# Moving the hi and lo halves of split operands, and the sums of exponentials, in a hand-ordered attention and MoE kernel

## The chip, the core and the metric

The kernel runs on one core of one Trainium2 chip. Its time is the device time of one execution in microseconds (us). TensorE (PE) multiplies matrices; its weight loads are listed apart as PEld. VectorE (DVE), ScalarE (ACT) and GpSimd (POOL) do the elementwise work, and SyncE (SP) issues the DMAs. Each engine works through its own instructions in order, and an instruction waits on semaphores until what it needs has been done by the others.

## The reference

Attention over pooled keys and values comes first, then a gated MoE layer with a third weight matrix:

```python
k_p = k.reshape(B, H, Sp, 8, D).mean(axis=3)          # B 8, H 8, S 576, D 64, Sp 72
v_p = v.reshape(B, H, Sp, 8, D).mean(axis=3)
scores = (1 / sqrt(D)) * q @ k_p^T
attn = exp(scores - max(scores)); attn = attn / (sum(attn) + 1e-9)
x = (attn @ v_p) as [B * S, H * D]                    # 4608 x 512
a = x @ w1; b = x @ w2                                # 512 x 1024 each
out = ((a * b) @ w3) @ w_out                          # 1024 x 1024, 1024 x 512
```

All inputs and the output are float32.

## The kernel before

**Split operands.** PE multiplies operands in a rounded form of float32 (`F32R`). For accuracy an operand is split into a hi part, which is a cast, and a lo part, which is the operand minus its hi part. A product is then three matmuls: hi times hi, hi times lo, lo times hi (`PASSES`). The cast runs on ACT, the subtraction on DVE, or on POOL for most blocks of w1 and w2. `split` (L151 to 153) issues both, one right behind the other. The same pair is written out for the transposed probabilities (`pt_post`, L486 and 487), for x (`av_post`, L510 and 511), for the product g = a * b (`b_post` L546 and `g_lo` L551), and for the leftover keys (`soft3`, L451 and 453).

**Stages.** First w3 and w_out are converted and multiplied into one matrix W (`w_mm`, L586). Then the 4608 tokens pass in 12 chunks of 384. For each chunk and each of 8 column blocks j, PE makes a = x w1 (`a_mm`), b = x w2 (`b_mm`, both L525), and adds g W to three accumulators (`out_mm`, L560). ACT copies a out of PSUM (`a_post`, L535), and DVE multiplies it with b (`b_post`, L545). Beside the MoE of one chunk the attention of the next is made. A chunk has three tiles of 128 tokens, or four of 96. Per tile the steps are: scores in two halves of four heads (`s_mm`, L404); minimum, subtraction, exponential and sum (`soft1`, L420 to 430); normalization (`soft2`, L439 to 442); leftover keys R (`soft3`); transposes of E and R on PE (`pt_mm` L464, `ptr_mm` L474); their copies (`pt_post`, `ptr_post`). Per pair of heads the product with the values follows (`av_mm`, L499 to 502). In five early tiles (`SOFT_ACT`) ACT makes exponential and sum in one (L430); all other tiles sum on DVE (L426).

**Weights.** The raw words of w1 and w2 are converted beside the first MoE chunk: L135 on ACT, L140 and L148 on DVE, then the split into `hl` (L152, L153).

**PSUM.** Five banks hold accumulators (`a`, `b`, `o0` to `o2`). Three banks, all called `att`, serve everything else: scores, transposes, attention products. A bank is free for the next use when its last reader is done.

**What sets the order.** A hand-written plan. `at(kind, k, fn, ...)` enters a step for slot k; a slot is about one group of MoE matmuls. The steps are sorted by the whole number of the slot, then by kind (loads L, elementwise steps P, MoE matmuls M, attention matmuls A), then by the fraction of k, then by entry. The sorted steps are issued one by one, so the order on each engine follows from the plan. `K0` is the slot 20, `M0` the slot 36 of the first MoE matmul.

Of the kernel before, what the change touches and what calls it, by code (L numbers as in the profile page):

```python
# [12 lines left out]
ALU = mybir.AluOpType  # L13
AX = mybir.AxisListType
# [4 lines left out]
def kernel(  # L19
# [14 lines left out]
    nc = tc.nc  # L34
# [3 lines left out]
    P = 128  # L38
# [3 lines left out]
    KR = KP - KM  # L42
# [45 lines left out]
    def f(ap):  # L88
        return ap.bitcast(F32)
# [56 lines left out]
    def conv_b(r, z):  # L146

        nc.vector.scalar_tensor_tensor(  # L148
            out=r, in0=z.bitcast(I32), scalar=3, in1=r, op0=ALU.logical_shift_left, op1=ALU.bitwise_or)

    def split(src, hi, lo, eng=nc.vector):  # L151
        nc.scalar.copy(out=hi, in_=src)  # L152
        eng.tensor_tensor(out=lo, in0=src, in1=f(hi), op=ALU.subtract)  # L153
# [207 lines left out]
    def pool_tree(t, dst):  # L361
        nc.gpsimd.tensor_tensor(out=t[:, :, 0:4], in0=t[:, :, 0:4], in1=t[:, :, 4:8], op=ALU.add)  # L362
        nc.gpsimd.tensor_tensor(out=t[:, :, 0:2], in0=t[:, :, 0:2], in1=t[:, :, 2:4], op=ALU.add)  # L363
        nc.gpsimd.tensor_tensor(out=dst, in0=t[:, :, 0], in1=t[:, :, 1], op=ALU.add)
# [12 lines left out]
    def prep_vr(b):  # L377
        m = p1.tile([P, 2, D], F32, tag="vrm", name="vrm")
        hi = p1.tile([P, 2, D], F32R, tag="vrh", name="vrh")
        pool_tree(stage.pop(("vr", b)), m)  # L380
        nc.scalar.copy(out=hi, in_=m)

        nc.scalar.activation(out=f(hi), in_=f(hi), func=AF.Copy, scale=msk[:, 0:1])
        nc.scalar.activation(out=m, in_=m, func=AF.Copy, scale=msk[:, 1:2])
        stage["vrp", b] = f(hi), m
# [25 lines left out]
    def soft1(n, t, half):  # L411

        b, off, nt = tok_tiles(n)[t]
        if half == 0:
            Et[n, t] = p2.tile([P, H, KP], F32, tag="E", name="E")
            Mt[n, t] = [p2.tile([P, H], F32, tag=tag, name=tag) for tag in ("mx", "sm")]
        E, (mx, sm) = Et[n, t], Mt[n, t]
        hs = slice(4 * half, 4 * half + 4)
        sv = Sp.pop((n, t, half))[:nt, :4 * KP].rearrange("p (h k) -> p h k", k=KP)
        nc.vector.tensor_reduce(out=mx[:nt, hs], in_=sv, axis=AX.X, op=ALU.min)  # L420
        if (n, t) not in SOFT_ACT:
            nc.vector.tensor_tensor(  # L422
                out=E[:nt, hs], in0=sv,
                in1=mx[:nt, hs].unsqueeze(2).broadcast_to([nt, 4, KP]), op=ALU.subtract)
            nc.scalar.activation(out=E[:nt, hs], in_=E[:nt, hs], func=AF.Exp, scale=-1.0)  # L425
            nc.vector.reduce_sum(out=sm[:nt, hs], in_=E[:nt, hs], axis=AX.X)  # L426
            return
        for i in range(4):
            h = 4 * half + i
            nc.scalar.activation(  # L430
                out=E[:nt, h], in_=sv[:, i], func=AF.Exp, scale=-1.0, bias=mx[:nt, h:h + 1],
                accum_out=sm[:nt, h:h + 1])
# [3 lines left out]
    def soft2(n, t):  # L436
        b, off, nt = tok_tiles(n)[t]
        E, sm = Et[n, t], Mt.pop((n, t))[1]
        nc.vector.tensor_scalar(  # L439
            out=sm[:nt], in0=sm[:nt], scalar1=1e-9, scalar2=float(POOL), op0=ALU.add, op1=ALU.mult)  # L440
        nc.vector.reciprocal(out=sm[:nt], in_=sm[:nt])
        nc.vector.tensor_tensor(
            out=E[:nt], in0=E[:nt], in1=sm[:nt].unsqueeze(2).broadcast_to([nt, H, KP]), op=ALU.mult)

    def soft3(n, t):
        b, off, nt = tok_tiles(n)[t]
        E = Et[n, t]
        R = Rt[n, t] = p2.tile([P, NPR, 2, 2, 2, KR], F32R, tag="R", name="R")
        er = E[:nt].rearrange("p (a h) (x e) -> p a (h x) e", h=2, e=KR)[:, :, 0:18:17, :]
        for dup in range(2):  # L450
            nc.scalar.copy(out=R[:nt, :, :, dup, 0], in_=er)  # L451
        for dup in range(2):
            nc.vector.tensor_tensor(
                out=R[:nt, :, :, dup, 1], in0=er, in1=f(R[:nt, :, :, dup, 0]), op=ALU.subtract)
# [23 lines left out]
    def pt_post(n, t):  # L478
        b, off, nt = tok_tiles(n)[t]
        if t == 0:  # L480
            PTh[n] = p1.tile([P, NPR, CH], F32R, tag="PTh", name="PTh")
            PTl[n] = p1.tile([P, NPR, CH], F32R, tag="PTl", name="PTl")
            PTr[n] = p1.tile([P, 2, CH], F32R, tag="PTr", name="PTr")
        pv = Tp.pop((n, t))
        hi, lo = PTh[n][:, :, off:off + nt], PTl[n][:, :, off:off + nt]
        nc.scalar.copy(out=hi, in_=pv[:, :, :nt])  # L486
        nc.vector.tensor_tensor(out=lo, in0=pv[:, :, :nt], in1=f(hi), op=ALU.subtract)

    def ptr_post(n, t):
        b, off, nt = tok_tiles(n)[t]  # L490
# [14 lines left out]
    def av_post(n, pr):  # L505
        if pr == 0:
            xT[n] = [xp.tile([P, NK, CH], F32R, tag=f"xT{s}", name=f"xT{s}") for s in range(2)]
        ps = Tp.pop((n, pr, "x"))[:, :CH]
        xh, xl = xT[n][0][:, pr], xT[n][1][:, pr]
        nc.scalar.copy(out=xh, in_=ps)  # L510
        nc.vector.tensor_tensor(out=xl, in0=ps, in1=f(xh), op=ALU.subtract)  # L511
# [28 lines left out]

    def b_post(m, j):
        g, ps = gt[m, j]
        gh = p2.tile([P, CH], F32R, tag="gh", name="gh")
        gl = p2.tile([P, CH], F32R, tag="gl", name="gl")
        nc.vector.tensor_tensor(out=g, in0=ps[:, :CH], in1=g, op=ALU.mult)  # L545
        nc.scalar.copy(out=gh, in_=g)  # L546
        gt[m, j] = (g, gh, gl)

    def g_lo(m, j):
        g, gh, gl = gt[m, j]  # L550
        nc.vector.tensor_tensor(out=gl, in0=g, in1=f(gh), op=ALU.subtract)  # L551
# [43 lines left out]


    plan = []

    def at(kind, k, fn, *args):


        plan.append((k // 1, "LPMA".index(kind), k % 1, len(plan), fn, args))

    def plan_att(n, s_at, ds, pt_at, av_at):


# [147 lines left out]
```

## Time and profile before

| | |
|---|---|
| median of 3 runs | 806.71 us (804.27 to 809.61) |
| profiled execution | 805.16 us, span 803.4 us |
| busy | PE 97%, PEld 90%, DVE 54%, ACT 36%, POOL 24% |
| mean granted clock of PE | 0.989 |
| first MoE matmul | 86.74 us after the start of the span |

A line of the profile names the source line, the engine, the operation, and the tiles as out<-in. In a timeline the first number is the start and the second the duration, in us; in square brackets stands how long the engine was idle just before and what ended that. In a group the count is followed by the busy time in us, the mean in ns, and the idle time before. A stretch A:B gives the busy time of PE, PEld, DVE, ACT and POOL, each with its number of instructions, then the clock granted to PE as a share of full speed, the DMA share and GB/s.

### The profile page before, as it was taken

The page shows a single profiled execution, that of the slowest core. Times are in us where ns is not written, and L with a number is a line of the kernel's source. Part 1 is how long each engine was busy: PE and PEld are TensorE (multiplying, and loading weights), DVE is VectorE, ACT ScalarE, POOL GpSimd, SP SyncE. Part 2 cuts the span into 40 slices and gives each one's busy share as a digit, 9 for nine tenths or more (in the row PEclk, how much of TensorE's full clock was granted, in tenths as well). Part 3 has the DMA queues.
Part 4 walks back from the last instruction along what each step waited for, and adds up shares of the span by engine and source line. Part 5 has one row for each costly group of instructions (what it writes and reads, how often), then busy time and mean ns, then how long its engine had stood idle before and what let it go on. Part 6 is the DMA issues. An engine that isn't in the chain of part 4 may idle for free.

```text
span 803.4 us, 11625 instructions
## 1 busy us (share of the span) xinstructions
PE 777.9 (97%) x4344; PEld 722.2 (90%) x4344; DVE 431.7 (54%) x873; ACT 288.0 (36%) x727; POOL 196.1 (24%) x234
## 2 busy tenths in 40 slices
PE   7899888999999999999999999999999999999998
PEld 6677777899999999999999999999999999999997
DVE  6968989465373375374374374474454455452112
ACT  5567565332243233242242333232242332332211
POOL 2155465107007302025008102034028020000000
PEclk8999999999999999999999999999999999999999
DMA  9988960045034030062043030071143110100101
GB/s 333 267 206 217 273 145 1 1 94 123 1 72 120 27 80 1 1 143 75 1 95 109 27 67 1 17 157 44 43 85 91 53 26 1 40 1 1 40 1 39
DMA packets 106632, 62.63 MB, mean 78 GB/s; under 512 B 73680, under 2 KB 90320, under 8 KB 106576
## 3 DMA queue, kind: packets, MB, share of 16 engines
q1 hardware_dynamic: 106576, 61.89, 30.1%
q8 instruction: 34, 0.56, 0.3%
q14 instruction: 22, 0.18, 0.1%
HBM read 52.43 MB, written 9.44 MB: 77 GB/s over the span
## 4 chain that ended last, share of the span: by engine, by line
PE 85%; DVE 7%; DMA 4%; issue 2%; ACT 2%; SPq 0%; DVEq 0%
PE o L560 24%; PE a L525 24%; PE b L525 23%; PE att L404 4%; PE o L586 2%; DMA st<-in_k_dram 2%; PE att L464 2%; DVE wb L140 1%; DVE wb L148 1%; PE att L501 1%; PE att L500 1%; PE att L502 1%; PE att L499 1%; PE att L474 1%; DMA raw<-in_moe_w_out_dram 1%
## 5 line engine op out<-in xcount | busy, mean ns | idle before, releaser
L525 PE MATMUL a<-xT,hl 128*128 128x384 f32 x1152 | 223.1, 342 | 0.0
L525 PE MATMUL b<-xT,hl 128*128 128x384 f32 x1152 | 220.3, 339 | 0.4 <-DVE Wc L153 0.4
L525 PEld LDWEIGHTS a<-xT,hl 128*128 128x128 f32 x1152 | 205.0, 190 | 4.9 <-POOL hl L153 0.2
L525 PEld LDWEIGHTS b<-xT,hl 128*128 128x128 f32 x1152 | 198.7, 188 | 0.8 <-DVE Wc L153 0.8
L560 PE MATMUL o<-Wc,gh 128*128 128x512 f32 x576 | 183.6, 400 | 0.0
L560 PEld LDWEIGHTS o<-Wc,gh 128*128 128x128 f32 x576 | 105.1, 189 | 17.3
L545 DVE TENSOR_TENSOR a<-b,a 128x384 f32<-128x384 f32 x96 | 53.1, 553 | 123.5 <-PE b L525 123.5
L362 POOL TENSOR_TENSOR st<-st 72x512 f32<-72x512 f32 (+1 forms) x53 | 73.0, 1377 | 173.2 <-DMA st<-in_k_dram 161.0
L560 PE MATMUL o<-Wc,gl 128*128 128x512 f32 x288 | 114.0, 396 | 0.0
L535 ACT COPY a<-a 128x384 f32<-128x384 f32 x96 | 46.1, 480 | 179.9 <-PE a L525 160.6
L546 ACT CAST gh<-a 128x384 fp32r<-128x384 f32 x96 | 49.2, 512 | 148.4 <-DVE a L545 148.4
L551 DVE TENSOR_TENSOR gl<-a,gh 128x384 fp32r<-128x384 f32 x96 | 59.4, 619 | 35.8 <-ACT gh L546 35.4
L375 POOL TENSOR_TENSOR vbd<-vm,vbd 64x256 fp32r<-64x256 f32 x16 | 13.3, 833 | 249.8 <-ACT vbd L374 248.2
L560 PEld LDWEIGHTS o<-Wc,gl 128*128 128x128 f32 x288 | 54.1, 188 | 12.5
L511 DVE TENSOR_TENSOR xT<-att,xT 128x384 fp32r<-128x384 f32 x48 | 26.5, 556 | 70.0 <-ACT xT L510 70.0
L426 DVE TENSOR_REDUCE sm<-E 128x4 f32<-128x288 f32 (+1 forms) x70 | 31.6, 451 | 46.3 <-ACT E L425 46.3
L404 PE MATMUL att<-kbd,qT 128*128 128x144 f32 (+1 forms) x320 | 52.1, 286 | 0.2 <-ACT E L430 0.2
L420 DVE TENSOR_REDUCE mx<-att 128x4 f32<-128x288 f32 (+1 forms) x80 | 36.0, 450 | 28.8 <-PE att L404 28.7
L425 ACT ACTIVATE E<-E 128x288 f32<-128x288 f32 (+1 forms) x70 | 31.1, 445 | 55.4 <-DVE E L422 55.4
L404 PEld LDWEIGHTS att<-kbd,qT 128*128 128x128 f32 (+1 forms) x320 | 46.6, 179 | 1.1 <-ACT E L430 0.5
L586 PE MATMUL o<-hl 128*128 128x512 f32 x144 | 42.3, 430 | 3.3 <-DVE hl L177 3.3
L363 POOL TENSOR_TENSOR st<-st 72x256 f32<-72x256 f32 (+1 forms) x53 | 41.8, 789 | 4.2
(87 smaller groups left out, 806.4 us busy)
## 6 DMA issues: line engine op xcount, KB each, us to landing
raw<-in_moe_w_dram SPq DMA_DIRECT2D x32, 512.0 KB
st<-in_k_dram SPq DMA_DIRECT2D x32, 288.0 KB
out_dram<-ob SPq DMA_DIRECT2D x35, 256.0 KB
st<-in_v_dram SPq DMA_DIRECT2D x32, 256.0 KB
qs<-in_q_dram SPq DMA_DIRECT2D x128, 48.0 KB
raw<-in_moe_w_out_dram SPq DMA_DIRECT2D x8, 512.0 KB
st<-in_v_dram SPq DMA_DIRECT2D x64, 64.0 KB
qs<-in_q_dram SPq DMA_DIRECT2D x96, 24.0 KB
```

Of the source, the lines that this page charges most:

```text
L362: nc.gpsimd.tensor_tensor(out=t[:, :, 0:4], in0=t[:, :, 0:4], in1=t[:, :, 4:8], op=ALU.add)
L363: nc.gpsimd.tensor_tensor(out=t[:, :, 0:2], in0=t[:, :, 0:2], in1=t[:, :, 2:4], op=ALU.add)
L404: nc.tensor.matmul(out=ps[:nt, 2 * KP * j:2 * KP * (j + 1)], lhsT=qT[n][:, pr, off:off + nt], rhs=kbd[b % 2][:, pr], start=True, stop=True,)
L420: nc.vector.tensor_reduce(out=mx[:nt, hs], in_=sv, axis=AX.X, op=ALU.min)
L426: nc.vector.reduce_sum(out=sm[:nt, hs], in_=E[:nt, hs], axis=AX.X)
L525: nc.tensor.matmul(out=o, lhsT=w12[j, w][sw][:, kt * P:(kt + 1) * P], rhs=x[sx][:, kt], start=(i == 0), stop=(i == 3 * NK - 1))
L535: nc.scalar.copy(out=a, in_=gt[m, j][:, :CH])
L545: nc.vector.tensor_tensor(out=g, in0=ps[:, :CH], in1=g, op=ALU.mult)
L546: nc.scalar.copy(out=gh, in_=g)
L551: nc.vector.tensor_tensor(out=gl, in0=g, in1=f(gh), op=ALU.subtract)
L560: nc.tensor.matmul(out=oacc[m][t], lhsT=(gh, gl)[sg][:, c], rhs=W[j][sw], start=(j == 0 and i == 0), stop=(j == NJ - 1 and i == 2))
L586: nc.tensor.matmul(out=wacc[h][it], lhsT=w3t[s][sa][:, it * P:(it + 1) * P], rhs=wo[j][sb], start=(j == 0 and i == 0), stop=(j == NJ - 1 a ...
```

## The change

The cast and the subtraction of a split become two steps. `late` issues the cast and stores the subtraction under a key; `lo` issues the stored subtraction where the plan says. This holds for w1 and w2, the transposed probabilities ("pt"), x ("x") and g ("g"). `soft3` is divided into casts (`soft3`) and subtractions (`soft4`), and `prep_vr` into additions on POOL and scalings on ACT (`prep_vr1`), which move to a later slot, as do the sums on POOL behind them. The two half sums of exponentials of a tile (L426) become one over all eight heads, issued in `soft2`. In the second chunk (n == 1) `soft2` and what follows it move by fractions of a slot. No matmul changes its place, nor any DMA.

```diff
+    def late(key, src, hi, lo, eng=nc.vector):
+        nc.scalar.copy(out=hi, in_=src)
+        los[key] = lo, src, f(hi), eng
+
+    def lo(*key):
+        sub(*los.pop(key))
...
-            nc.vector.reduce_sum(out=sm[:nt, hs], in_=E[:nt, hs], axis=AX.X)
             return
...
     def soft2(n, t):
+        if (n, t) not in SOFT_ACT:
+            nc.vector.reduce_sum(out=sm[:nt], in_=E[:nt], axis=AX.X)
...
     def b_post(m, j):
         g, ps = gt[m, j]
+        nc.vector.tensor_tensor(out=g, in0=ps[:, :CH], in1=g, op=ALU.mult)
+        gt[m, j] = g
+
+    def g_hi(m, j):
+        g = gt[m, j]
         gh = p2.tile([P, CH], F32R, tag="gh", name="gh")
         gl = p2.tile([P, CH], F32R, tag="gl", name="gl")
-        nc.vector.tensor_tensor(out=g, in0=ps[:, :CH], in1=g, op=ALU.mult)
-        nc.scalar.copy(out=gh, in_=g)
+        late(("g", m, j), g, gh, gl)
...
+    SL = (2, 3.1)
...
-            at("P", k + 2, soft2, n, t)
-            at("P", k + 3, soft3, n, t)
+            at("P", k + SL[n == 1], soft2, n, t)
+            at("P", k + 3 + 0.2 * (n == 1), soft3, n, t)
+            at("P", k + 3 + 0.45 * (n == 1), soft4, n, t)
...
+            at("P", k + 1 + 0.35 * (n == 1), lo, "pt", n, t)
...
-            at("P", av_at[pr] + 1, av_post, n, pr)
+            at("P", av_at[pr] // 1 + 1.1, av_post, n, pr)
+            at("P", av_at[pr] // 1 + 1.5, lo, "x", n, pr)
...
-        at("P", prep_r + 1, prep_vr2, b)
+        at("P", prep_r + 1.3, prep_vr1, b)
+        at("P", prep_r + 2.3, prep_vr2, b)
...
+            at("P", k + 4 + (0.75 if (j, w) in LO_DVE else 0), lo, "w12", j, w)
...
-            at("P", k + 2.5, g_lo, m, j)
+            at("P", k + 2.35, g_hi, m, j)
+            at("P", k + 2.9, lo, "g", m, j)
```

Three places show what that does to the queues. The first is DVE's queue when the first chunk's attention products come out, just ahead of the first MoE matmul. km is the fourth part of a batch's pooled keys, wb and raw belong to the conversion of w1 and w2, xT is x with its hi part as second input. Before:

```order
L319 TENSOR_REDUCE km<-st 72x128
L148 SCALAR_TENSOR_TENSOR wb<-wb 128x512
L511 TENSOR_TENSOR xT_980<-att,xT_979 128x384
L140 TENSOR_SCALAR wb<-raw 128x512
L153 TENSOR_TENSOR hl<-wb,hl 128x512
L511 TENSOR_TENSOR xT_980<-att,xT_979 128x384 x3
```

and now (all subtractions of a split have the line of `sub`, L152):

```order
L332 TENSOR_REDUCE km<-st 72x128
L148 SCALAR_TENSOR_TENSOR wb<-wb 128x512
L140 TENSOR_SCALAR wb<-raw 128x512
L152 TENSOR_TENSOR xT_982<-att,xT_981 128x384 x4
L152 TENSOR_TENSOR hl<-wb,hl 128x512
```

The first lo part of x has moved behind the conversion L140, and the other three ahead of the lo part of a block of w2.

The second place is DVE's queue at the end of the second chunk's attention, while the MoE of the first chunk is at j = 4. The scores' minimum mx and subtraction E are the last tile's second half. Before:

```order
L420 TENSOR_REDUCE mx<-att 96x4
L422 TENSOR_TENSOR E<-att,mx 96x288
L426 TENSOR_REDUCE sm<-E 96x4
L551 TENSOR_TENSOR gl<-a,gh 128x384
L439 TENSOR_SCALAR sm<-sm 96x8
L441 RECIPROCAL sm<-sm 96x8
L442 TENSOR_TENSOR E<-E,sm 96x576
L276 STREAM_TRANSPOSE qT<-qs 128x384
L487 TENSOR_TENSOR PTl<-att,PTh 128x4x96
L453 TENSOR_TENSOR R<-E,R 96x8x8 x2
```

and now:

```order
L437 TENSOR_REDUCE mx<-att 96x4
L439 TENSOR_TENSOR E<-att,mx 96x288
L152 TENSOR_TENSOR gl<-a,gh 128x384
L289 STREAM_TRANSPOSE qT<-qs 128x384
L152 TENSOR_TENSOR PTl<-att,PTh 128x4x96
L289 STREAM_TRANSPOSE qT<-qs 128x384
L456 TENSOR_REDUCE sm<-E 96x8
L457 TENSOR_SCALAR sm<-sm 96x8
L459 RECIPROCAL sm<-sm 96x8
L460 TENSOR_TENSOR E<-E,sm 96x576
L152 TENSOR_TENSOR R<-E,R 96x8x8 x2
```

The sum and the normalization have moved behind two transposes of q and the lo part of the third tile's probabilities, and R stands right behind the normalization.

The third place is ACT's queue at the same time. E are the last tile's exponentials in two halves, vrh and vrm the leftover values' scalings, gh the cast of g for j = 4. Before:

```order
L451 CAST R<-E 96x8x8 x2
L425 ACTIVATE E<-E 96x288
L381 CAST vrh<-vrm 128x128
L383 ACTIVATE vrh<-vrh,msk 128x128
L384 ACTIVATE vrm<-vrm,msk 128x128
L546 CAST gh<-a 128x384
L425 ACTIVATE E<-E 96x288
L152 CAST hl<-wb 128x512 x2
L486 CAST PTh<-att 128x4x96
```

and now (all casts of `late` have the line L162):

```order
L442 ACTIVATE E<-E 96x288
L471 CAST R<-E 96x8x8 x2
L442 ACTIVATE E<-E 96x288
L162 CAST hl<-wb 128x512
L398 CAST vrh<-vrm 128x128
L400 ACTIVATE vrh<-vrh,msk 128x128
L401 ACTIVATE vrm<-vrm,msk 128x128
L162 CAST gh<-a 128x384
L162 CAST hl<-wb 128x512
L162 CAST PTh<-att 128x4x96
```

The cast of g has moved behind the second half's exponential, a cast of a weight block and the three scalings.

More of the change, by code (lines that the diff above doesn't have):

```diff
@@ L149, in conv_b, with sub @@
             out=r, in0=z.bitcast(I32), scalar=3, in1=r, op0=ALU.logical_shift_left, op1=ALU.bitwise_or)
+    def sub(out, a, b, eng=nc.vector):
+        eng.tensor_tensor(out=out, in0=a, in1=b, op=ALU.subtract)
     def split(src, hi, lo, eng=nc.vector):
         nc.scalar.copy(out=hi, in_=src)
-        eng.tensor_tensor(out=lo, in0=src, in1=f(hi), op=ALU.subtract)
+        sub(lo, src, f(hi), eng)
+    los = {}
+    def late(key, src, hi, lo, eng=nc.vector):
[3 more added lines that the diff above has]
+        sub(*los.pop(key))
     def w_tiles(s):
@@ L236, in w12_split @@
         w12[j, w] = hl_cell(FREED[2 * j + w])
-        split(f(r), *w12[j, w], eng=nc.vector if (j, w) in LO_DVE else nc.gpsimd)
+        late(("w12", j, w), f(r), *w12[j, w], eng=nc.vector if (j, w) in LO_DVE else nc.gpsimd)
     def pieces(n):
@@ L380, in prep_vr, with prep_vr1 @@
         pool_tree(stage.pop(("vr", b)), m)
+        stage["vrp", b] = hi, m
+    def prep_vr1(b):
+        hi, m = stage.pop(("vrp", b))
         nc.scalar.copy(out=hi, in_=m)
@@ L443, in soft2, with rest_keys, soft4 @@
             out=E[:nt], in0=E[:nt], in1=sm[:nt].unsqueeze(2).broadcast_to([nt, H, KP]), op=ALU.mult)
+    def rest_keys(n, t):
+        nt = tok_tiles(n)[t][2]
+        return Et[n, t][:nt].rearrange("p (a h) (x e) -> p a (h x) e", h=2, e=KR)[:, :, 0:18:17, :]
     def soft3(n, t):
-        b, off, nt = tok_tiles(n)[t]
-        E = Et[n, t]
+        nt = tok_tiles(n)[t][2]
         R = Rt[n, t] = p2.tile([P, NPR, 2, 2, 2, KR], F32R, tag="R", name="R")
-        er = E[:nt].rearrange("p (a h) (x e) -> p a (h x) e", h=2, e=KR)[:, :, 0:18:17, :]
         for dup in range(2):
-            nc.scalar.copy(out=R[:nt, :, :, dup, 0], in_=er)
+            nc.scalar.copy(out=R[:nt, :, :, dup, 0], in_=rest_keys(n, t))
+    def soft4(n, t):
+        nt = tok_tiles(n)[t][2]
+        R = Rt[n, t][:nt]
         for dup in range(2):
-            nc.vector.tensor_tensor(
-                out=R[:nt, :, :, dup, 1], in0=er, in1=f(R[:nt, :, :, dup, 0]), op=ALU.subtract)
+            sub(R[:, :, :, dup, 1], rest_keys(n, t), f(R[:, :, :, dup, 0]))
     Tp = {}
@@ L484, in pt_post @@
         pv = Tp.pop((n, t))
-        hi, lo = PTh[n][:, :, off:off + nt], PTl[n][:, :, off:off + nt]
-        nc.scalar.copy(out=hi, in_=pv[:, :, :nt])
-        nc.vector.tensor_tensor(out=lo, in0=pv[:, :, :nt], in1=f(hi), op=ALU.subtract)
+        hi, lo_ = PTh[n][:, :, off:off + nt], PTl[n][:, :, off:off + nt]
+        late(("pt", n, t), pv[:, :, :nt], hi, lo_)
     def ptr_post(n, t):
@@ L509, in av_post @@
         xh, xl = xT[n][0][:, pr], xT[n][1][:, pr]
-        nc.scalar.copy(out=xh, in_=ps)
-        nc.vector.tensor_tensor(out=xl, in0=ps, in1=f(xh), op=ALU.subtract)
+        late(("x", n, pr), ps, xh, xl)
     PASSES = ((0, 0), (0, 1), (1, 0))
@@ L542, in b_post @@
         g, ps = gt[m, j]
+        nc.vector.tensor_tensor(out=g, in0=ps[:, :CH], in1=g, op=ALU.mult)
+        gt[m, j] = g
+    def g_hi(m, j):
+        g = gt[m, j]
         gh = p2.tile([P, CH], F32R, tag="gh", name="gh")
         gl = p2.tile([P, CH], F32R, tag="gl", name="gl")
-        nc.vector.tensor_tensor(out=g, in0=ps[:, :CH], in1=g, op=ALU.mult)
-        nc.scalar.copy(out=gh, in_=g)
+        late(("g", m, j), g, gh, gl)
         gt[m, j] = (g, gh, gl)
-    def g_lo(m, j):
-        g, gh, gl = gt[m, j]
-        nc.vector.tensor_tensor(out=gl, in0=g, in1=f(gh), op=ALU.subtract)
     def out_mm(m, j):
```

## The prediction

> **What bounds it now.** I read the page first: TensorE (PE) is busy for 97% of the span, VectorE (DVE) for 54%. The waits and the stages then say where that 97% leaves something to move. Waits of PE between 80 and 145 us, the only ones after 80 us:
>
> ```profile
> PE 777.9 (97%) x4344; PEld 722.2 (90%) x4344; DVE 431.7 (54%) x873; ACT 288.0 (36%) x727; POOL 196.1 (24%) x234
> ```
>
> ```profile
> PE att L474 <- ACT E L430: 4.7, 2, 3.9
> PE att L474 <- DVE E L422: 2.0, 1, 2.0
> PE att L474 <- DVE R L453: 1.7, 1, 1.7
> PE att L499 <- DVE xT L511: 1.6, 1, 1.6
> PE att L328 <- DVE km L319: 1.6, 1, 1.6
> PE b L525 <- DVE Wc L153: 0.4, 1, 0.4
> ```
>
> They make 12.0 us. Busy times of two stretches (us; PE, PEld, DVE, ACT, POOL, granted clock):
>
> ```profile
> 92.00:144.00 52.00, 41.87 (x224) 38.25 (x222) 47.81 (x75) 27.70 (x88) 29.86 (x26) 0.93 0.44 92
> 144.00:803.40 659.40, 655.49 (x3707) 617.38 (x3707) 310.99 (x675) 201.21 (x492) 131.96 (x163) 1.00 0.21 51
> ```
>
> So there are two kernels in one. From 144 us on PE runs without a wait for 659.4 us, and nothing that DVE does sooner can shorten that. From 92 to 144 us (first MoE chunk, attention of the second, and conversion of w1 and w2) DVE is busy for 47.81 of 52 us and PE only for 41.87. The last of PE's waits shows where the two meet, in order of time (start, duration):
>
> ```profile
> 141.74 2.09 DVE L453 TENSOR_TENSOR R<-E,R 96x64 fp32r<-96x64 f32 x2
> ...
> 143.97 0.36 PE L474 MATMUL att<-ident,R 96*128 96x96 f32 x2 [1.73 <-DVE R L453]
> ```
>
> I call this the gate: the transposes of R of the second chunk's last tile. PE's own work is the same before and after, in the same order. The new time is therefore the old one plus the shift of the gate, as long as PE does not wait behind it. The other waits lie ahead of the gate, and shortening them alone gives nothing. What counts is the length of DVE's queue up to R.
>
> **Part 1: the attention products of chunk 0.** Rows from 77 to 84 us:
>
> ```profile
> 77.71 0.41 DVE L140 TENSOR_SCALAR wb<-raw 128x512 int32<-128x512 int32 x1
> ...
> 82.47 1.55 POOL L362 TENSOR_TENSOR st<-st 72x512 f32<-72x512 f32 x1 [2.40 <-DMA st<-in_k_dram]
> 82.78 0.55 DVE L511 TENSOR_TENSOR xT<-att,xT 128x384 fp32r<-128x384 f32 x1
> 83.25 1.05 DVE L140 TENSOR_SCALAR wb<-raw 128x512 int32<-128x512 int32 x1
> ...
> 83.39 0.44 PE L499 MATMUL att<-PTh,vbd 128*128 128x384 f32 x1 [1.60 <-DVE xT L511]
> ```
>
> The fourth product waits for the first lo part of xT, which reads its PSUM bank last. That lo part now stands behind the L140. L140 takes 0.41 alone, but it took 1.05 beside POOL's addition and ended at 84.30, 0.28 after POOL's (82.47 + 1.55 = 84.02). Starting earlier it should end there again, so the lo part starts at 84.3, not 82.78: 1.5 us. Some 0.2 comes back, since the three other lo parts no longer stand behind the split of w2. I take **+1.3**; bounds +0.4 (L140 unhindered) and +1.5. The first a, the casts of W behind it and DVE, which waits for these, move along.
>
> The Trainium skill ("SBUF — State Buffer", Who interferes with whom) says that GpSimd shares a pair of SBUF ports with VectorE, locked for a whole instruction; tensor_scalar and operations with two SBUF inputs can want it, tensor_reduce never does. The L140 above agrees; by that rule the end at 84.3 holds, and the longer sum of part 2 is not stretched.
>
> **Part 2: DVE's queue from 92 us to the gate.** What goes are waits of DVE:
>
> ```profile
> DVE sm L426 <- ACT E L425: 2.0, 4, 0.5
> ...
> DVE gl L551 <- ACT gh L546: 0.9, 1, 0.9
> DVE wb L148 <- ACT wb L135: 0.8, 1, 0.8
> ```
>
> Each half tile's sum waited 0.5 for its exponentials; now other work stands between. **-3.7**, and what takes their place is priced anew below. Groups of DVE instructions from 92 to 144 us (count | busy, mean ns):
>
> ```profile
> L148 DVE SCALAR_TENSOR_TENSOR wb<-wb 128x512 int32<-128x512 int32 x11 | 11.6, 1052 | 0.9 <-ACT wb L135 0.8
> L140 DVE TENSOR_SCALAR wb<-raw 128x512 int32<-128x512 int32 x10 | 8.9, 890 | 0.0
> L442 DVE TENSOR_TENSOR E<-E,sm 96x576 f32<-96x576 f32 x4 | 4.7, 1164 | 0.1
> ...
> L426 DVE TENSOR_REDUCE sm<-E 96x4 f32<-96x288 f32 x4 | 1.8, 449 | 2.0 <-ACT E L425 2.0
> ...
> L276 DVE STREAM_TRANSPOSE qT<-qs 128x384 f32<-128x384 f32 x2 | 1.1, 564 | 0.0
> ```
>
> ```profile
> 96.30 0.67 DVE L148 SCALAR_TENSOR_TENSOR wb<-wb 128x512 int32<-128x512 int32 x1
> ...
> 118.86 0.76 DVE L442 TENSOR_TENSOR E<-E,sm 96x576 f32<-96x576 f32 x1
> ```
>
> Four sums of 288 (0.45 each) become two of 576. No row has that shape. Its bounds are 0.45 and 0.90; I take 0.75, by L442's 576 elements undisturbed: 2 x 0.75 - 4 x 0.45 = **-0.3**. One more transpose of q stands ahead of R: **+0.56**.
>
> New waits come from ScalarE (ACT), whose cast of g (gh) moves behind other work of its slot. ACT's groups from 92 to 144 us, then single rows:
>
> ```profile
> L152 ACT CAST hl<-wb 128x512 fp32r<-128x512 f32 x13 | 7.9, 616 | 0.0
> L135 ACT ACTIVATE wb<-raw 128x512 f32<-128x512 f32 x9 | 6.1, 672 | 0.0
> ...
> L546 ACT CAST gh<-a 128x384 fp32r<-128x384 f32 x5 | 2.6, 516 | 3.4 <-DVE a L545 3.4
> ...
> L425 ACT ACTIVATE E<-E 96x288 f32<-96x288 f32 x4 | 1.8, 444 | 8.5 <-DVE E L422 8.5
> L451 ACT CAST R<-E 96x64 fp32r<-96x64 f32 x8 | 1.6, 246 | 5.9 <-DVE E L442 5.9
> ```
>
> ```profile
> 111.53 0.32 ACT L430 ACTIVATE E<-att,mx 96x72 f32<-96x72 f32 x1 [2.73 <-DVE mx L420]
> ...
> 112.64 0.20 ACT L430 ACTIVATION_READ_ACCUMULATOR E<-att,mx 96x1 f32 x1
> ...
> 133.94 0.28 ACT L381 CAST vrh<-vrm 128x128 fp32r<-128x128 f32 x1
> ...
> 134.56 0.39 ACT L384 ACTIVATE vrm<-vrm,msk 128x128 f32<-128x128 f32 x1
> ```
>
> - lo of g(1): behind E come an exponential 0.44, an L135 0.67 and gh 0.52 on ACT, 1.6; on DVE one L140 covers 0.4 to 0.9: wait 1.0.
> - g(2): four exponentials 1.3 (111.53 to 112.84) and gh 0.5, covered by an L148 0.7: 1.0. Behind it the lo part of PT waits for its cast, which stands behind gh, L135 and an L152: 0.7.
> - g(3): the same, covered by an L148 and an L140: 0.6.
> - g(4): exponential 0.44, L152 0.62, the three scalings of vr 1.0 (133.94 to 134.95), gh 0.52, with nothing between on DVE: 2.6.
> - R of tiles 0, 2 and 3 now stands right behind E's scaling and waits for its own cast: 0.25 and 0.2 of handover, 1.4 in all.
>
> Together **+7.3**. Behind a waiting lo part everything of DVE queues up, the sums and R of the gate too.
>
> Against this stands POOL, busy for 29.86 of these 52 us. DVE's SBUF operations run longer beside it: L148 11 x (1.05 - 0.67), L140 10 x (0.89 - 0.41), L442 4 x (1.16 - 0.76), 10.6 us in these three. While DVE waits, POOL's work gets done, and stretches the next rows less. The added idle time is 7.3 - 3.7 = 3.6. Bounds 0 (POOL has nothing ready) and -7 (two thirds of the stretch); I take one for one, **-3.6**.
>
> **The rest.** Chunks 2 to 11 get the same moves. Their cover is the idle half of DVE; a later lo of g has this margin:
>
> ```profile
> 167.49 0.55 DVE L551 TENSOR_TENSOR gl<-a,gh 128x384 fp32r<-128x384 f32 x1
> ...
> 172.62 0.72 PE L560 MATMUL o<-Wc,gh 128*128 128x512 f32 x2
> ```
>
> It ends 4.6 us before its use, and is moved by under a slot of PE: nothing. POOL's VR sums a slot later and the hi casts bunched are not on the way. SP's queue is unchanged.
>
> **Sum.** 1.3 - 3.7 - 0.3 + 0.56 + 7.3 - 3.6 = +1.6 on the profiled execution's 805.16 (span 803.4 and 1.76 around it): **806.8**. The median shown, 806.71, is 1.55 above that execution; measured from there it would be 808.3. Under 1% (8 us) I count as no change.
>
> **A clock that could fall.** Three stretches of 3.41 or 4 us:
>
> ```profile
> 130.42:133.83 3.41, 1.45 (x11) 1.07 (x10) 3.10 (x6) 0.24 (x1) 1.91 (x3) 1.00 0.00 0
> ...
> 134.00:138.00 4.00, 4.00 (x16) 4.00 (x16) 3.39 (x8) 2.96 (x9) 2.26 (x5) 0.59 0.02 4
> ...
> 140.66:144.07 3.41, 1.68 (x11) 1.25 (x10) 3.41 (x6) 1.22 (x4) 2.00 (x2) 1.00 0.00 0
> ```
>
> After a stretch with PE busy for 1.45 us the clock halved for 3.4 us, which costs 1.7; the wait at the gate, with 1.68, just escaped. Ahead of the gate such a fall is hidden, behind it it counts in full.
>
> The Trainium skill ("TensorE: Matmul & The Clock Gate", What's actually happening) lets the clock drop after at least one idle window of about 3.4 us. Here 2 us of idleness was enough, so the trace is stricter. By the page nothing would be added at the gate, and rival B would be 810.4.
>
> **Rivals.**
> - A, faster: ACT, idle for half of this stretch, serves the casts in time. Then the 7.3 goes, and POOL may still interfere less: 1.3 - 3.7 - 0.3 + 0.56 = -2.1, with 3.4 of relief -5.5: **799.7**. For it speaks ACT's 27.70 of 52 us, against it that ACT is served in order and gh stands behind casts that wait for DVE. PE's waits of 12.0 cap it.
> - B, slower: POOL has nothing to do in DVE's new pauses, which come while ACT still makes its inputs. Relief 0: +5.2; and the wait before the gate, longer by the pause at g(4), leaves PE busy for under 1.5 of 3.4 us: +1.7. **812.1**. It decides where lo of g(4) ends more than 3 us later than now.
> - C: in later chunks a bank or a lo part comes late and PE waits 1 us in each of 11 chunks: 806.8 + 11 = **817.8**. Only the margin above speaks, against it.
>
> **Chances.** Forecast 0.60 (802 to 810), A 0.22 (796 to 802), B 0.14 (810 to 814), C 0.04. The range 798 to 812 leaves out a quarter of A, half of B and C, under 0.2. Faster by over 1%: 0.07, the lower third of A; slower by over 1%: 0.05, C and a sliver of B; within: 0.88.
>
> **What would show it.** Right: the sums' wait is gone, lo of g waits over 2 us at g(4), PE's fourth product starts about 1.5 us later than its cue, R of the last tile ends at 145 to 146, and no wait of PE follows. Wrong: R ends before 142 (A) or after 148 (B), or PE waits after 200 us (C).

## The result and the profile after

The changed kernel takes 800.58 us (median of 10 runs, 796.16 to 803.34) against 806.30 us for the kernel before on the same chip: a ratio of **0.9922, 95% interval 0.9901 to 0.9944**. It is faster by 0.8%, less than the 1% that I had called a change, but surely not the same, and not slower as forecast.

The page of the kernel after, busy times of the engines:

```profile
PE 778.0 (97%) x4344; PEld 721.4 (90%) x4344; DVE 418.9 (52%) x838; ACT 285.6 (36%) x727; POOL 195.5 (24%) x234
```

The stretches from the first a to the gate, and from the gate to the end (columns as before: PE, PEld, DVE, ACT, POOL, clock). Before:

```profile
86.74:143.97 57.23, 46.66 (x250) 42.65 (x249) 52.04 (x82) 32.95 (x98) 31.07 (x26) 0.94 0.50 116
143.97:803.40 659.43, 655.51 (x3707) 617.41 (x3707) 311.02 (x675) 201.21 (x492) 131.96 (x163) 1.00 0.21 51
```

and after:

```profile
88.88:140.79 51.91, 44.60 (x250) 39.19 (x249) 44.46 (x80) 32.95 (x98) 29.84 (x25) 1.00 0.48 100
140.79:800.20 659.41, 655.51 (x3707) 617.47 (x3707) 307.80 (x641) 199.02 (x493) 131.63 (x164) 1.00 0.21 51
```

Behind the gate nothing changed: 659.43 and 659.41. The stretch ahead of it became 5.32 shorter. DVE is busy there for 7.58 less (52.04 to 44.46) and idle for 2.26 more (5.19 to 7.45). ACT does the same work, POOL nearly. PE, busy for 2.06 less with the same matmuls, was granted the full clock throughout. PE's waits from the first a to the gate, after:

```profile
PE att L487 <- DVE E L460: 2.8, 3, 2.2
PE att L341 <- DVE km L332: 1.6, 1, 1.6
PE att L497 <- DVE R L152: 1.5, 4, 0.7
...
PE b L546 <- DVE Wc L152: 0.6, 1, 0.6
```

Where PE waited 4.7 and 2.0 for the exponentials and the subtraction, and 1.7 for R at the gate, it now waits 2.8 for the normalized E, and 1.5 for R, spread over four places. The end of the second chunk's attention, in order of time (DVE, and two rows of PE):

```profile
135.15 0.83 DVE L152 TENSOR_TENSOR gl<-a,gh 128x384 fp32r<-128x384 f32 x1 [2.35 <-ACT gh L162]
...
137.32 0.70 DVE L456 TENSOR_REDUCE sm<-E 96x8 f32<-96x576 f32 x1
...
140.11 0.52 PE L487 MATMUL att<-ident,E 96*128 96x96 f32 x4 [2.18 <-DVE E L460]
140.28 0.37 DVE L152 TENSOR_TENSOR R<-E,R 96x64 fp32r<-96x64 f32 x2 [0.31 <-ACT R L471]
...
140.79 0.36 PE L497 MATMUL att<-ident,R 96*128 96x96 f32 x2 [0.16 <-DVE R L152]
```

The wait of 2.35 at g(4) is there, as forecast, and still the gate comes 3.2 us earlier. R, which took 2.09, takes 0.37. DVE still comes last here: where PE waited 1.73 for R, it waits 2.18 for the normalized E, just ahead of the gate, and 0.16 for R.

Two more stretches belong to the account. From the first attention product of chunk 0 to the first a it was 7.24 us (79.50 to 86.74) and is 5.24 (83.64 to 88.88). Ahead of that product the change moves little, but single executions differ there by several us: it starts between 76.73 and 83.64 us in the 14 profiles of this study, without order by kernel. So I compare profiles from that product on. There the change brings 2.00 + 5.32 + 0.02 = 7.3 us; the medians say 5.7 (4.5 to 8.0 by the interval).

### The profile page after: what moved, and what is told of

The parts are those of the page before. It is cut to its first block, busy times and chain, and to the rows that moved or that the text cites. A ratio compares the mean times of both kernels' runs of the same rounds, so it can differ in the third digit from the quotient of the medians.

```text
span 800.2 us, 11632 instructions
## 1 busy us (share of the span) xinstructions
PE 778.0 (97%) x4344; PEld 721.4 (90%) x4344; DVE 418.9 (52%) x838; ACT 285.6 (36%) x727; POOL 195.5 (24%) x234
## 4 chain that ended last, share of the span: by engine, by line
PE 84%; DMA 6%; DVE 4%; ACT 2%; POOL 2%; SPq 1%; issue 1%; DVEq 0%; POOLq 0%; ACTq 0%
PE o L581 24%; PE a L546 24%; PE b L546 24%; PE att L421 4%; DMA raw<-in_moe_w_dram 2%; PE att L487 2%; PE o L607 2%; DMA st<-in_k_dram 1%; PE att L523 1%; PE att L522 1%; PE att L524 1%; PE att L521 1%; DMA raw<-in_moe_w_out_dram 1%; PE att L497 1%; ACT E L446 1%
## 5 line engine op out<-in xcount | busy, mean ns | idle before, releaser
L546 PE MATMUL a<-xT,hl 128*128 128x384 f32 x1152 | 220.1, 339 | 0.0
L546 PEld LDWEIGHTS a<-xT,hl 128*128 128x128 f32 x1152 | 202.1, 188 | 4.9 <-POOL hl L152 0.2
L152 DVE TENSOR_TENSOR gl<-a,gh 128x384 fp32r<-128x384 f32 x96 | 60.1, 626 | 80.1 <-ACT gh L162 79.8
L162 ACT CAST gh<-a 128x384 fp32r<-128x384 f32 x96 | 48.7, 507 | 86.0 <-DVE a L564 86.0
L442 ACT ACTIVATE E<-E 128x288 f32<-128x288 f32 (+1 forms) x70 | 31.1, 444 | 91.1 <-DVE E L439 91.1
L152 DVE TENSOR_TENSOR xT<-att,xT 128x384 fp32r<-128x384 f32 x48 | 26.6, 557 | 68.9 <-ACT xT L162 68.8
L162 ACT CAST xT<-att 128x384 fp32r<-128x384 f32 x48 | 23.0, 479 | 61.0 <-PE att L524 61.0
```

Source lines behind the costliest of these rows:

```text
L152: eng.tensor_tensor(out=out, in0=a, in1=b, op=ALU.subtract)
L546: nc.tensor.matmul(out=o, lhsT=w12[j, w][sw][:, kt * P:(kt + 1) * P], rhs=x[sx][:, kt], start=(i == 0), stop=(i == 3 * NK - 1))
```

## The experiments

The first theories: S, the sums' part frees DVE's queue; G, the moved lo parts of g do; P, what shrinks is the stretching of DVE's instructions beside POOL; W, only waits for ACT count, and POOL doesn't matter. All kernels below are the kernel before with the edits named, unless said otherwise. "First part" is the time from the first attention product to the first a, "stretch" from there to the gate, "behind" from the gate to the end, in one profiled execution. A median is told with the ratio to the kernel before in the same series.

| kernel | median us | ratio [95%] | first part | stretch | behind |
|---|---|---|---|---|---|
| before | 806.0 to 807.2 | 1 | 7.24 | 57.23 | 659.43 |
| after | 800.58 | 0.9922 [0.9901, 0.9944] | 5.24 | 51.91 | 659.41 |
| 1 sums' part | 799.4 | 0.9913 [0.9880, 0.9947] | 6.68 | 51.69 | 659.34 |
| 2 g alone | 805.72 | 0.9994 [0.9971, 1.0017] | 7.23 | 56.58 | 659.42 |
| 3 x and w1, w2 | 807.04 | 1.0006 [0.9985, 1.0028] | 8.10 | 56.72 | 662.06 |
| 4 pt and VR | 801.5 | 0.9937 [0.9916, 0.9957] | 5.04 | 54.74 | 659.39 |
| 5 before, less POOL work | 801.93 | 0.9954 [0.9937, 0.9971] | 7.22 | 52.67 | 661.28 |
| 6 after, less POOL work | 798.5 | 0.9905 [0.9880, 0.9931] | 5.69 | 50.56 | 659.73 |
| 7 VR alone | 800.92 | 0.9931 [0.9909, 0.9953] | 5.12 | 55.39 | 659.38 |
| 8 sums, pt, VR | 799.35 | 0.9914 [0.9889, 0.9939] | 5.04 | 52.65 | 660.97 |
| 9 VR, first batch | 804.7 | 0.9982 [0.9959, 1.0005] | 5.04 | 57.40 | 661.00 |
| 10 VR, later batches | 803.38 | 0.9957 [0.9937, 0.9976] | 7.21 | 55.36 | 659.39 |
| 11 one sum | 801.72 | 0.9940 [0.9914, 0.9966] | 6.72 | 53.20 | 659.40 |
| 12 later slots | 800.6 | 0.9928 [0.9900, 0.9957] | 6.62 | 53.50 | 659.35 |

### Which part of the change brings it

**1. The sums' part:** one sum per tile, and the later slots of the second chunk.

```diff
-            nc.vector.reduce_sum(out=sm[:nt, hs], in_=E[:nt, hs], axis=AX.X)
...
+        if (n, t) not in SOFT_ACT:
+            nc.vector.reduce_sum(out=sm[:nt], in_=E[:nt], axis=AX.X)
...
-            at("P", k + 2, soft2, n, t)
+            at("P", k + SL[n == 1], soft2, n, t)
```

(and the fractions of `soft3` and `soft4`)

> Before with only the sums part: one sum over eight heads in the normalization step, and in the second chunk that step and R a fraction of a slot later. Measure beside the time: the stretch from the first MoE matmul to the gate (57.2 us in before, 51.9 in the changed kernel). Theory S (the sums part frees DVE's queue: the four waits of 0.5 us go, and R no longer stands between POOL's operations): the stretch shrinks by 3 to 5 us, time 801 to 803. Theory G (the gain comes from the lo parts of g, out of the way behind other work): the stretch shrinks by under 1.5 us, time 805 to 807.

Measured: 0.9913, the whole of what the change brings. S holds. The stretch is as short as after:

```profile
89.87:141.56 51.69, 45.54 (x251) 40.80 (x250) 45.92 (x81) 33.13 (x98) 29.81 (x26) 0.97 0.52 114
```

DVE is busy for 45.92 in it, 6.12 less than before, and idle for 5.77, only 0.58 more.

**2. The cast and the lo part of g alone.**

```diff
-            at("P", k + 2, g_hi, m, j)
-            at("P", k + 2.5, lo, "g", m, j)
+            at("P", k + 2.35, g_hi, m, j)
+            at("P", k + 2.9, lo, "g", m, j)
```

> Before with only the g part: cast of g at 0.35 and its lo part at 0.9 of the slot. Theory G: the stretch to the gate shrinks by 3 us or more, time 801 to 803. Theory S: it doesn't shrink, since new waits of the lo parts for their casts (4.3 us in the changed kernel) stand against less stretching: time 805 to 808.

Measured: no difference. G falls.

**3. The lo parts of x and of w1 and w2.**

```diff
-            at("P", av_at[pr] + 1, av_post, n, pr)
-            at("P", av_at[pr] + 1, lo, "x", n, pr)
+            at("P", av_at[pr] // 1 + 1.1, av_post, n, pr)
+            at("P", av_at[pr] // 1 + 1.5, lo, "x", n, pr)
...
+            at("P", k + 4 + (0.75 if (j, w) in LO_DVE else 0), lo, "w12", j, w)
```

> Before with only the x part (four casts together, four lo parts together) and the lo parts of the three DVE blocks of w1 and w2 three quarters of a slot later. My prediction's term: the first MoE matmul 1.3 us later, time 807 to 808. Rival: the other lo parts, now together, free the banks for the transposes of q sooner, and what L140 costs is lost in the state of POOL at that moment: within 0.7 us of before.

Measured: no difference in the median; the first part is 0.86 longer. Timeline of this kernel, DVE and POOL, where my Part 1 lay:

```profile
81.67 0.42 DVE L140 TENSOR_SCALAR wb<-raw 128x512 int32<-128x512 int32 x1
82.00 1.48 DVE L152 TENSOR_TENSOR xT<-att,xT 128x384 fp32r<-128x384 f32 x3
...
82.35 1.29 POOL L375 TENSOR_TENSOR st<-st 72x512 f32<-72x512 f32 x1 [3.38 <-DMA st<-in_k_dram]
```

The L140 was done before POOL's addition began, and took 0.42: of my bounds, +0.4 and +1.5, the lower one came true, since the fourth product waits 1.90 for xT instead of 1.60, 0.30 more. The other 0.56 comes behind that product, where the clock fell. From there to the first a it was 3.35 us at a granted clock of 1.00 before, and in this kernel:

```profile
82.61:86.52 3.91, 3.91 (x16) 3.39 (x17) 3.20 (x6) 1.25 (x3) 2.21 (x3) 0.69 1.09 271
```

**4 and 7. The lo part of pt with the move of the leftover values (VR), then VR alone.** Number 7 has the last two lines only.

```diff
+            at("P", k + 1 + 0.35 * (n == 1), lo, "pt", n, t)
...
-        at("P", prep_r, prep_vr1, b)
-        at("P", prep_r + 1, prep_vr2, b)
+        at("P", prep_r + 1.3, prep_vr1, b)
+        at("P", prep_r + 2.3, prep_vr2, b)
```

> Before with only the lo parts of the transposed probabilities later in the second chunk and the scalings and POOL sums of the leftover values later in all batches. Prediction: these cost nothing, time within 1 us of before. Rival: the scalings no longer stand in front of ACT's cast of g and of the exponentials while POOL still adds, so the stretch to the gate shrinks by 1 to 3 us.

> Before with the leftover values' scalings and POOL sums later, alone (the lo parts of the probabilities stay). If the scalings, which stood on ACT in front of the copies of the transposed probabilities and of the cast of g, made the gain of the fourth run: time 801 to 803, the stretch to the gate 2 to 3 us shorter. If the lo parts of the probabilities made it: within 1.5 us of before.

Measured: 0.9937 and 0.9931. The move that I had priced at nothing brings nearly as much as the sums, and in number 7 it shows in two places: 2.1 in the first part, 1.8 in the stretch. The profile from the first product on gives 4.0, the median 5.1. The lo part of pt adds nothing that the medians show.

**8. The sums' part, pt and VR together,** that is the kernel after without the moves of g, x and w1, w2.

> The changed kernel without its g part and without its x and w1/w2 part: sums, lo parts of the probabilities, scalings. If the gains add up: 796 us or less. If both remove the same thing, the time before the gate being bounded by DVE's own work: 798 to 801, as the sums alone.

Measured: 0.9914. The two gains don't add up: in the stretch the sums alone give 5.5, VR alone 1.8, both with pt 4.6. On top of the sums, VR and pt bring nothing that the medians show. Here the moves of g, x and w1, w2 are left out without a loss that could be measured.

### Where VR works

For this the theories were Q (ahead of the first MoE matmul), R (in the stretch) and N (mostly chance).

**9 and 10. VR moved for the first batch only, then for the seven others only.**

```diff
-        at("P", prep_r, prep_vr1, b)
-        at("P", prep_r + 1, prep_vr2, b)
+        at("P", prep_r + 1.3 * (b == 0), prep_vr1, b)
+        at("P", prep_r + 1 + 1.3 * (b == 0), prep_vr2, b)
```

(number 10 with `b > 0`)

> The scalings of the leftover values and the sums on POOL come later for the first batch only (before the first MoE matmul); the other seven batches stay as before. Theory Q (the gain of the values' part arises ahead of the first MoE matmul: casts of the first probabilities pass the scalings, and POOL's sums leave the conversion alone there): the first a comes 2 us earlier after the first attention product than before (5.0 to 5.7 instead of 7.2), the stretch from the first a to the gate keeps its 57 us, and the median falls by 2 to 5 us. Theory R (it arises in that stretch, from the second batch, whose scalings stand ahead of the cast of g in ACT's queue at 134 us): no change here, within 1.5 us of before. Theory N (the single difference of 5 us was mostly chance in the part ahead of the first attention product): both this and the other half within 2 us of before.

> The same move for the other seven batches only; the first batch stays as before. Theory Q: the stretch from the first attention product to the first a keeps its 7.2 us, and the median is within 1.5 us of before. Theory R: the stretch from the first a to the gate falls from 57.2 to 55 us or less, the median by 2 to 5 us. Theory N: within 2 us of before.

Measured: each half does one of the two things, and only that one. The first batch shortens the first part (7.24 to 5.04) and leaves the stretch; the others shorten the stretch (57.23 to 55.36) and leave the first part. So Q and R are both right, each for its half, and N falls for number 10, whose median is 3.8 lower than before; against N in number 9, 2.5 lower, speak mainly the parts of the profile. The ratios, 0.9982 and 0.9957, make 0.6% together, near number 7's 0.7%. The interval of number 9 still holds no difference; its profile lost 1.6 behind the gate to the clock (below).

How the first part shrinks: timeline of the kernel before (POOL, then DVE)

```profile
78.37 1.70 POOL L153 TENSOR_TENSOR hl<-wb,hl 128x512 fp32r<-128x512 f32 x1 [0.64 <-ACT hl L152]
...
78.83 1.52 DVE L140 TENSOR_SCALAR wb<-raw 128x512 int32<-128x512 int32 x1
80.27 1.99 DVE L319 TENSOR_REDUCE km<-st 72x128 f32<-72x1024 f32 x1
```

and of number 9 (POOL, DVE, PE):

```profile
77.45 1.48 POOL L152 TENSOR_TENSOR hl<-wb,hl 128x512 fp32r<-128x512 f32 x1
...
77.10 0.68 DVE L140 TENSOR_SCALAR wb<-raw 128x512 int32<-128x512 int32 x1
77.69 2.02 DVE L332 TENSOR_REDUCE km<-st 72x128 f32<-72x1024 f32 x1
...
80.84 0.44 PE L520 MATMUL att<-PTh,vbd 128*128 128x384 f32 x1
```

The first product starts at 79.50 before and at 78.56 in number 9. The reduction km, which stands ahead of the first lo part of x, begins 0.77 after it before and 0.87 ahead of it now. The L140 in front of km started ahead of POOL's subtraction instead of behind it and took 0.68 instead of 1.52. That is 0.84 of the 1.64 by which km comes earlier; the rest lies in rows farther ahead and was not traced. The fourth product's wait of 1.60, from which my Part 1 started, is gone.

How the stretch shrinks: POOL beside R of the last tile, before

```profile
141.75 0.78 POOL L375 TENSOR_TENSOR vbd<-vm,vbd 64x256 fp32r<-64x256 f32 x1 [1.48 <-ACT vbd L374]
142.49 1.25 POOL L153 TENSOR_TENSOR hl<-wb,hl 128x512 fp32r<-128x512 f32 x1
```

and in number 10 (POOL, then DVE, then PE):

```profile
136.48 2.48 POOL L409 TENSOR_TENSOR VR<-vrh,vrm 32x128 fp32r<-32x128 f32 x4
139.03 1.29 POOL L152 TENSOR_TENSOR hl<-wb,hl 128x512 fp32r<-128x512 f32 x1
140.28 0.74 POOL L388 TENSOR_TENSOR vbd<-vm,vbd 64x256 fp32r<-64x256 f32 x1
...
138.42 0.61 DVE L152 TENSOR_TENSOR R<-E,R 96x64 fp32r<-96x64 f32 x2
...
139.61 0.33 PE L496 MATMUL att<-ident,R 96*128 96x96 f32 x2
```

Before, the two subtractions of R ran beside those of vbd and hl on POOL and took 2.09; with VR's sums later, vbd comes behind R, and R, now beside the last of VR's sums, takes 0.61. The scaling of E two steps ahead of R took 0.75 as well, where it took 1.57 before. PE's transposes of R then don't wait: DVE is no longer what comes last at the gate. The Trainium skill ("SBUF — State Buffer", Who interferes with whom) has GpSimd and VectorE share a pair of ports that one instruction keeps to its end. The trace agrees: this pair of subtractions of two SBUF operands takes 2.09 beside two POOL instructions, and 0.37 in the kernel after (at 140.28), where POOL stands still from 139.36 to 140.99.

### What POOL's stretching is worth

**5 and 6. Less work on POOL,** in the kernel before and in the kernel after. For the second batch's values the first two of three additions are left out, so its pooled values, and the output rows that use them, aren't those of the reference.

```diff
-    def pool_tree(t, dst):
+    def pool_tree(t, dst, short=False):
+        if not short:
-        nc.gpsimd.tensor_tensor(out=t[:, :, 0:4], in0=t[:, :, 0:4], in1=t[:, :, 4:8], op=ALU.add)
-        nc.gpsimd.tensor_tensor(out=t[:, :, 0:2], in0=t[:, :, 0:2], in1=t[:, :, 2:4], op=ALU.add)
+            nc.gpsimd.tensor_tensor(out=t[:, :, 0:4], in0=t[:, :, 0:4], in1=t[:, :, 4:8], op=ALU.add)
+            nc.gpsimd.tensor_tensor(out=t[:, :, 0:2], in0=t[:, :, 0:2], in1=t[:, :, 2:4], op=ALU.add)
...
-        pool_tree(stage.pop(("vr", b)), m)
+        pool_tree(stage.pop(("vr", b)), m, short=b == 1)
```

(and the same for `prep_v`)

> Before, with two of the three POOL additions left out when the values of batch 1 are pooled (three tiles; its pooled values are not the reference's): 8.7 us less POOL work between the first MoE matmul and the gate, while DVE's and ACT's instructions stay the same in the same order. Theory P (DVE's queue is long because its SBUF operations are held up by POOL's, so relief from POOL is what the change brought): DVE is busy 3 to 6 us less in this stretch and the stretch shrinks by as much, from 57.2 to 51 to 54 us. Theory W (waits for ACT and the order alone set the length): under 1 us.

> The changed kernel with the same additions left out. Theory P: less is left to win, since DVE's pauses already take POOL's work: the stretch of 51.9 us shrinks by 0.5 to 2.5 us, less than in before. Theory W: under 1 us, as in before.

The stretch in number 5, then in number 6:

```profile
88.45:141.12 52.67, 44.78 (x250) 40.95 (x249) 47.25 (x82) 32.94 (x98) 23.92 (x20) 0.97 0.54 119
```

```profile
85.81:136.37 50.56, 44.43 (x250) 39.27 (x249) 43.50 (x80) 32.97 (x98) 23.72 (x21) 1.00 0.64 143
```

With 7.15 less of POOL's work the kernel before has a stretch 4.56 shorter, and DVE, with the same instructions in the same order, is busy for 4.79 less. That much of DVE's 52 us was stretching by these additions alone. In number 5 too DVE comes last at the gate, and PE waits 2.42 for R there. In the kernel after, 6.12 less of POOL's work gives only 1.35: most of it no longer hurts there. P stands, W falls.

### Which half of the sums' part

Theories: S1, one sum instead of two; S2, the later slots.

**11. One sum, slots of before,** then **12. half sums, later slots.** Number 11 has the first three changed lines of number 1, number 12 the others.

> The two half sums of a tile become one in the step of the normalization, all other steps of the second chunk in their slots of before. Theory S1 (the gain of the sums' part is the shorter work and the vanished waits for the exponentials of a half): the stretch from the first a to the gate falls from 57.2 to 53 or less and the median by 4 to 7 us. Theory S2 (the gain lies in the later slots of the second chunk, where DVE finds the exponentials done): the sum now waits for the second half's exponential right behind it, the waits for exponentials keep 1 to 2 us, the stretch falls by 1.5 us at most and the median by under 2.

> The half sums stay where they were, and only the normalization and the leftover keys of the second chunk move by fractions of a slot, behind the second half's exponential. Theory S1: the half sums still wait 2.0 us in all for their exponentials; the stretch from the first a to the gate falls by 1.5 us at most and the median by under 2. Theory S2: the stretch falls to 53 us or less and the median by 4 to 7 us.

Measured: either half alone brings most of it, 4.0 and 3.7 in the stretch, 0.9940 and 0.9928 in the medians; together 5.5 and 0.9913. Waits of DVE in number 12:

```profile
DVE sm L443 <- ACT E L442: 2.1, 4, 0.6
...
DVE R L152 <- ACT R L470: 1.3, 3, 0.6
```

There the half sums wait as before, 2.1 in all, and R waits 1.3 more, and the stretch is 3.7 shorter all the same. S1 and S2 both fall as exclusive theories. The stretch in number 11, then in number 12:

```profile
84.90:138.10 53.20, 45.05 (x251) 41.07 (x249) 50.71 (x80) 32.85 (x98) 31.56 (x28) 0.97 0.62 146
83.35:136.85 53.50, 45.38 (x250) 40.58 (x249) 46.71 (x83) 33.24 (x99) 34.30 (x28) 0.97 0.54 129
```

The two halves work differently. Against before, with 52.04 busy and 5.19 idle, DVE in number 11 is idle for 2.7 less and busy for 1.3 less: mostly waits that go. In number 12 it is idle for 1.6 more and busy for 5.3 less: the later order alone takes the stretching away, with POOL busy for more, not less. Which single meetings with POOL the later slots avoid was not traced.

## Why the prediction was wrong

**What held.** The new time is the old one plus the shift of the gate: the time behind it was 659.41 after, and 659.34 to 659.73 us in eight of the twelve experiments, whatever was done ahead of it; in the other four the clock fell behind the gate (last section). No later chunk waited, so rival C is out. The sum of 576 took 0.72 (I took 0.75), by the groups of DVE in the stretch after:

```profile
L148 DVE SCALAR_TENSOR_TENSOR wb<-wb 128x512 int32<-128x512 int32 x12 | 9.4, 786 | 0.0
L140 DVE TENSOR_SCALAR wb<-raw 128x512 int32<-128x512 int32 x11 | 8.5, 777 | 0.0
...
L152 DVE TENSOR_TENSOR gl<-a,gh 128x384 fp32r<-128x384 f32 x5 | 3.1, 622 | 4.3 <-ACT gh L162 4.3
...
L152 DVE TENSOR_TENSOR R<-E,R 96x64 fp32r<-96x64 f32 x8 | 1.7, 253 | 1.5 <-ACT R L471 1.3
...
L456 DVE TENSOR_REDUCE sm<-E 96x8 f32<-96x576 f32 x2 | 1.4, 718 | 0.0
```

The same groups before:

```profile
L148 DVE SCALAR_TENSOR_TENSOR wb<-wb 128x512 int32<-128x512 int32 x12 | 12.2, 1020 | 0.9 <-ACT wb L135 0.8
L140 DVE TENSOR_SCALAR wb<-raw 128x512 int32<-128x512 int32 x11 | 9.3, 847 | 0.0
...
L453 DVE TENSOR_TENSOR R<-E,R 96x64 fp32r<-96x64 f32 x8 | 3.9, 527 | 0.0
```

**-3.7, waits that go:** the sums' 2.0 and wb's 0.8 are gone, as said.

**+7.3, new waits:** 4.3 for the cast of g and 1.3 for R, 5.6. At g(4) 2.35 against my 2.6, R 1.3 against 1.4; PT and g(3), 0.7 and 0.6, did not wait. Nearly right, 1.7 too high. But these waits look paid back. Number 8, without the moves of g, x and w1, w2, waits 0.2 for the cast of g where the kernel after waits 4.3, and its stretch is 0.74 longer, since DVE is busy for 47.31 in it, against 44.46 after. Number 2 says less: with the moved cast alone DVE waits only 1.8 for it.

**-3.6, POOL's relief: the step that failed by size.** It measured about twice that. DVE's busy time fell by 7.58; without the sums (-0.3) and the transpose (+0.56), counted apart, that is -7.8, beyond even my bound of -7. With -7.8 in place of -3.6 my sum is -2.6: this term alone turns its sign. I had counted only three groups as stretched (L148, L140, L442), and let relief grow one for one with DVE's pauses. In number 1 the pauses grew by 0.58 and the busy time fell by 6.12. What the rows show is a matter of which instruction meets which: R's eight subtractions, which my 10.6 us left out, went from 3.9 to 1.7 us, L148's from 12.2 to 9.4. POOL's busy time is nearly the same (31.07 and 29.84), so its work must now fall more on DVE's pauses and on instructions that it doesn't hold up; this was not counted row by row. In my account of the stretch, idle +3.6 and busy -3.3 made +0.3; measured are +2.3 and -7.6, -5.3.

**"The rest": the step that failed in kind.** "POOL's VR sums a slot later and the hi casts bunched are not on the way." Numbers 7, 9 and 10 show that VR's move was on the way twice. In the kernel before it is worth 2.1 us ahead of the first MoE matmul, and 1.9 at the gate, where I had quoted R's 2.09 us without asking which POOL instruction stood beside it. The scalings stand in ACT's queue ahead of casts, and the sums in POOL's ahead of vbd; I had priced neither queue. With the sums' part in place the medians show no gain from it (0.9913 without VR and pt in number 1, 0.9914 with them in number 8), so of the two steps it is the relief, more than VR, that made the result differ.

**+1.3, Part 1:** alone it was +0.86 (number 3), 0.30 of it the longer wait behind an unhindered L140, the rest the fallen clock. In the kernel after, VR's first batch takes that and more away: 5.24 after and 5.04 in number 8, without this part, so there it costs 0.2.

**"Shortening the waits ahead of the gate alone gives nothing"** held as long as DVE came last: in number 2 PE had the full clock and busy time of 44.23 in the stretch, 2.4 less than before, and the stretch became only 0.65 shorter, since PE waited 2.4 at the gate. But in numbers 1, 7, 10, 11 and 12 PE reached the gate without a wait, and then its earlier waits and its clock decide: PE, not DVE, is the floor there. The gains don't add up in part because numbers 1 and 7 both take away the same wait of 1.73 at the gate. In number 8 DVE comes last again, having waited 1.9 for a cast of pt, and PE waits 2.21 for the normalized E. In the kernel after DVE comes last too, so a sum along its queue was the right account there; its terms were wrong.

**Rivals.** The result lies in the band of A (796 to 802, chance 0.22), and near its 799.7. R ended at 140.65, before the 142 that I had named as A's sign. But that A came so near is luck in the main: ACT did not serve the casts in time, DVE waited 5.6 for them, and POOL's relief was over twice A's 3.4. Rival B's wait at g(4) came, its slower end did not.

## What to carry to other kernels

A step is off the critical path only when its neighbours on other engines are too: for each long row at the point that decides, look up which POOL instruction ran beside it, and what each moved step does to that meeting. A row that is three times as long as its like (2.09 against 0.6 for R) is a term of its own, to be priced by place and not as a mean over a stretch. And once the last wait at such a point is gone, the next engine's earlier waits begin to count, so gains of parts measured alone are bounds and not terms of a sum.

## What the runs showed of the hardware

I had written that after a stretch of 3.41 us with PE busy for 1.45 the clock halved, and that the wait at the gate, with 1.68, "just escaped". That bound does not stand. The 3.41 us ahead of the gate and the 3.4 behind it (the number after POOL is the clock), in number 9:

```profile
137.59:141.00 3.41, 1.68 (x10) 1.23 (x9) 3.41 (x6) 1.23 (x4) 2.00 (x2) 1.00 0.00 0
141.00:144.40 3.40, 3.40 (x14) 3.40 (x15) 2.76 (x6) 1.61 (x4) 0.73 (x1) 0.64 0.00 0
```

and in number 2:

```profile
141.07:144.48 3.41, 0.61 (x5) 0.40 (x5) 3.41 (x6) 1.62 (x5) 2.15 (x3) 1.00 0.00 0
144.48:147.89 3.41, 3.41 (x21) 3.41 (x22) 2.76 (x6) 1.59 (x4) 0.58 (x1) 1.00 0.00 0
```

With 1.68 us the clock fell, and the time behind the gate grew by 1.6; with 0.61 it did not. Numbers 3, 5 and 8 fell as well (2.6, 1.9 and 1.5 behind the gate). The kernel before had 1.69 in the last 3.41 us and did not fall. Nearest alike are the kernel after and number 8, here in this order:

```profile
137.38:140.79 3.41, 1.08 (x7) 0.51 (x6) 3.00 (x8) 0.79 (x3) 1.95 (x2) 1.00 0.00 0
140.79:144.20 3.41, 3.40 (x21) 3.41 (x22) 2.53 (x5) 2.12 (x6) 2.23 (x2) 1.00 0.00 0
...
131.72:135.13 3.41, 1.04 (x8) 0.48 (x6) 3.00 (x7) 0.80 (x3) 1.94 (x2) 1.00 0.00 0
135.13:138.54 3.41, 3.41 (x12) 3.41 (x13) 2.73 (x5) 1.74 (x5) 2.21 (x2) 0.51 0.00 0
```

So the amount of work in the last 3.41 us alone doesn't decide, and what else does, no run here settles. That the profiles before and after show the same time behind the gate is luck in this respect: either could have lost some 1.5 us there. The Trainium skill ("TensorE: Matmul & The Clock Gate", What's actually happening) asks for at least one idle window of about 3.4 us for a fall. The trace doesn't agree: number 9, which waited only 1.73 us at the gate, fell with less.

The size of the meetings of DVE and POOL was the other surprise: two additions fewer per tile of one batch's values on POOL, an engine busy for 24% of the span, made the kernel before faster by 0.46% (0.9954, 0.9937 to 0.9971), more than half of what the whole change brings.
